# Two attentions on one core: output products one step behind a block's end, and the step with two maxima moved onto the block's end

## The chip, the core and the metric

The kernel runs on one core of a Trainium2 chip. The metric is device microseconds from launch to end. TensorE multiplies into PSUM, which has eight banks of 128 x 512 fp32; VectorE and ScalarE read PSUM and empty its banks; GpSimd works between tiles in SBUF; SyncE's queue issues almost all transfers. In the rows of a profile these are PE (PEld is the load of its weights), DVE, ACT, POOL and SP.

## What is computed

Two independent attentions over 2048 positions, each with 32 heads of 18 values (D = 576), in fp32. Attention A looks back at 8 positions, 2 apart; attention B looks at all. Their outputs stand side by side.

```python
def _A_ref(x, wqkv, wo):                      # H = 32, Dh = 18, W = 8, dil = 2
    q, k, v = ...                             # x @ wqkv, split by head
    idx = pos[:, None] - (jnp.arange(W) * dil)[None, :]
    logits = jnp.einsum("bhsd,bhswd->bhsw", q, k_at_idx) * scale
    logits = jnp.where(idx >= 0, logits, -1e9)
    o = jnp.einsum("bhsw,bhswd->bhsd", softmax(logits), v_at_idx)
    return o.reshape(B, S, D) @ wo

def _B_ref(x, wqkv, wo):
    scores = jnp.einsum("bhqd,bhkd->bhqk", q, k) * scale
    o = jnp.einsum("bhqk,bhkd->bhqd", softmax(scores), v)
    return o.reshape(B, S, D) @ wo

return jnp.concatenate([a, b], axis=-1)
```

## The kernel before

**Three stretches.** For some 416 us both attentions' queries, keys and values are projected; A's go to DRAM (`da`), B's queries and keys too (`dqk`), split into a rounded part and a remainder so that fast products keep fp32's precision. Then comes a main loop of 512 steps (`while step < ALL`), and in its last 25 steps most of B's output projection.

**A step of the main loop.** B's heads are taken in 8 groups of 4 (`g`), the queries of a group in 4 blocks of 512 (`b`), the keys in 16 tiles of 128 (`kt`). Step `step` is one tile: `step = 16 * block + kt`. It does the following.

- *Scores*: four products of keys and queries, one per head (line 388), each into a bank of PSUM, two of them into two neighbouring banks called `pair`. ScalarE takes the exponential of each (line 398) or of the pair at once (line 401).
- *Maxima*: the largest score of each query, which the exponential needs, is found for a later block. Three further products (line 239) fill three banks, one of them in two parts; VectorE reduces each by one instruction (lines 256, 258 and 272). A block has 64 maxima to be taken. When the last of them is taken, two small instructions of VectorE (lines 282 and 290) put them into order.
- *Values*: `weigh` multiplies the exponentials of the *previous* step with the values (line 898), four heads side by side in the bank `po`. These four are the last that a step has on TensorE.

Scores and maxima use 64 rows of TensorE each and run in two halves side by side; the value products use all 128 rows.

**A block's end.** The value products of a block's last tile (kt = 15) stand at the end of the step behind it, which is kt = 0 of the next block. There `finish` has VectorE copy `po` into `o` (line 908). The value products of the next step (kt = 1) start `po` anew, so they wait for that copy. One step later SyncE's queue loads the denominators (`den<-o`, line 932), and further steps divide and store.

**Attention A in between.** A's eight pieces are worked out by GpSimd, some instructions of VectorE (maxima `am`, line 1059, four per piece) and ScalarE (exponents, line 1069, one whole or two halves), beside B's steps. Piece `j` starts at step 10 + 55 j; some 90 steps later it is stored to `dao`. Some steps then load half of a piece back (`at` and `ahl`, lines 1118 and 1120) and multiply it with A's output weights (line 1239): these are the *output products*. There are 27 of them in a step, into two banks; ScalarE copies one bank to `y` and VectorE adds the other (line 1142). A loaded half serves two steps with products. The tile `at` has one buffer, so the next load waits until the products on it are done.

**Which steps have products.** `TURNS` is a sorted list of steps at which products may stand: one in every block (`16 * n + AT`), one for each piece's exponents, and the eight in `MORE`. Each half takes the next two free turns; its load is issued 9 steps ahead of the first, or as soon as the buffer's last step with products is over. The steps taken are kept in the set `producing`. Exponents are taken in one piece if their step has products, and in two halves, the first one step earlier, if not.

**How many maxima.** `many` is 3 as a rule. A step with products takes two more. A step next to a block's end without products takes two only. Three and no products is the *plain* step, whose order is fixed (`PLAIN`); a step with products or with two maxima has its order set by `in_turn`, which plays two queues, one per half of TensorE's rows, against expected times of the engines. `behind()` raises `many` to 4 if the maxima come late; here it never does.

**Order.** The order of the instructions on each engine is the order in which the code issues them; no scheduler moves them. Each engine waits on semaphores where an operand or a buffer isn't ready. SyncE's queue is served in order too, so a transfer that waits holds up those behind it.

Of the kernel before, what the change touches and what calls it, by code (L numbers as in the profile page):

```python
# [40 lines left out]
EARLY_PAIRS = EARLY * NB * PIECES + 8  # L41
AHEAD = 7

AT = 0

MORE = (439, 441, 451, 467, 475, 477, 484, 486)

# [7 lines left out]

TURNS = sorted({NT * n + AT for n in range(1, 30)} | {A_FROM + GAP * j + 35 for j in range(NJ)} | set(MORE))

# [12 lines left out]
def two_attentions(ctx: ExitStack, tc, xa, wa, woa, xb, wb, wob, out):  # L70
# [45 lines left out]
    def pooled(apart_):  # L116

        nonlocal ring
        ring = "pool"
        n = 7 if apart_ else 5  # L120
        if apart_:
            pair_room()
            freed[5] = freed[6] = freed["pair"]
        rings.update({k: list(range(n)) for k in ("pool", "scores", "else")})

    def apart():

        nonlocal ring
        ring = "else"
        assert not held  # L130
        if len(rings["else"]) == 7:
            pair_room()
            freed["pair"] = max(freed[5], freed[6])
        n = sorted(range(5), key=lambda i: freed[i])
        rings["scores"] = [n[1], n[3]]
        rings["else"] = [n[0], n[2], n[4]]
# [44 lines left out]
    step = 0  # L181
# [8 lines left out]
    def due():  # L190
        for f in agenda.pop(step, []):
            f()
# [126 lines left out]
    given = [0, 0]  # L319
    projecting = True  # L320

    def maximum(r):

        given[r] += 1
        return blocks[find(lambda rest: rest[r])][1](r)
# [14 lines left out]
    def first_part(r):  # L340

        for i in range(2):
            given[i] += 0.5
        if open_parts:
            part, args = open_parts.pop()
        else:
            rest, _, part = blocks[find(lambda rest: rest[0] and rest[1] and rest[0][-1][0] > 1)]
            piece = rest[0].pop()
            assert rest[1].pop() == piece
            args = (0, *piece)  # L350
            open_parts.append((part, (1, *piece)))
        ps = bank()
        ins, _ = part(*args, r, ps)
        taken = rings[ring][-1]

        def second():
            if ring == "else":
                rings["else"].remove(taken)
                rings["else"].append(taken)
            return part(*args, 1 - r, ps, ins)[1]  # L360

        return second
# [7 lines left out]
    def score(g, b, kt, h, kind):  # L370

        assert (g, b) in placed
        qs, ks = sets[g % 3]
        p, r = divmod(h, 2)
        at = slice(64 * r, 64 * r + 56)
        if len(scored) == 4:
            scored.clear()
            counted[0] += 1
        parity = counted[0] % 2
        n = sum(k == kind for k in scored)  # L380
        scored.append(kind)
        if kind == "pair":
            if n == 0:
                both_scores[:] = [pair_of_banks()]
            ps = both_scores[0][:, 512 * n : 512 * n + 512]
        else:
            ps = bank("else" if projecting else "scores")
        nc.tensor.matmul(ps, ks[at, p, 128 * kt : 128 * kt + 128], qs[at, b, p], start=True, stop=True)  # L388
        filled(r, 226, ps if kind != "pair" else None if n else both_scores[0])
        if kind == "single":  # L390
            e = whole = (work if parity else e_room).tile([128, 512], F32, name=f"e{n}{parity}", bufs=1)
        else:
            if n == 0:
                both_es[:] = [e_room.tile([128, 1024], F32, name=f"ee{parity}", bufs=1)]
            whole = both_es[0]
            e = whole[:, 512 * n : 512 * n + 512]
        if kind != "pair":
            nc.scalar.activation(e, ps, AF.Exp, scale=SCALE)  # L398
            emptied("ACT", 490, r, ps)
        elif n:  # L400
            nc.scalar.activation(whole, both_scores[0], AF.Exp, scale=SCALE)  # L401
            emptied("ACT", 916, r, both_scores[0])
        return e
# [102 lines left out]
    def do_all(fs):  # L506
        for f in fs:
            f()
# [6 lines left out]
    with (tc.tile_pool(name="x", bufs=1, side="right") as xp,  # L515
# [367 lines left out]
        step = 0  # L883
# [106 lines left out]
    producing = set()  # L990
# [254 lines left out]
    def in_turn(queues):  # L1245

        while any(queues):
            at = []
            for r, q in enumerate(queues):
                need = q[0][0] if q else None  # L1250
                free = 0
                if need == "E":
                    free = parted_at[0]
                elif need == "pair":
                    free = 0 if "pair" in held else freed["pair"] + 165
                elif need:
                    free = min(freed[i] for i in rings[ring] if i not in held) + 165 if any(i not in held for i in rings[ring]) else 1e9
                at.append(max(busy[r], free) if q else 2e9)
            r = int(at[1] < at[0])
            busy[0], busy[1] = max(busy[0], at[r]), max(busy[1], at[r])  # L1260
            queues[r].pop(0)[1]()
# [109 lines left out]
    total = early + rest  # L1371

    def behind():

        most = 0
        for n in range(int(sum(given)) // (2 * PIECES), NG * NB):
            until = NT * n - AHEAD
            more = 3 * (until - step) + 2 * sum(step <= p < until for p in producing)
            most = max(most, 2 * PIECES * (n + 1) - int(sum(given)) - more)
        return most  # L1380
# [4 lines left out]
    while step < ALL:  # L1385
        n, kt = divmod(step, NT)
        g, b = divmod(n, NB)
        many = min(4 if behind() > 0 else 2 if kt == 1 and step > 1 and step - 1 not in producing else 3, total - int(sum(given)))
        if open_parts and total - int(sum(given)) < 3:
            many = 1  # L1390
        es = [None] * 4
        products = inside.pop(0)() if inside else ([], [])
        plain = many == 3 and not any(products)
        if not plain:
            pooled(any(products))
        parts = many == 3 or many == 1 and open_parts
        left = many - parts
        a = left // 2 if left != 1 or given[0] >= given[1] else 1
        b_ = left - a
        extra = any(products) and int(sum(given)) + many + 2 <= total  # L1400
        ops = {"D": lambda: parted.append(first_part(0)) or parted_at.insert(0, busy[0] + 250), "E": lambda: parted.pop()()(),
               "A": lambda: maximum(0)(), "B": lambda: maximum(1)(),
               "+": lambda: None,
               **{c: lambda h=i % 4, kind="single" if i < 4 else "apart" if any(products) else "pair": es.__setitem__(h, score(g, b, kt, h, kind))
                  for i, c in enumerate("0123wxyz")}}

        def queue(text, own):
            q = []
            for c in text:
                if c == "+":  # L1410
                    q += own
                    own = []
                elif c == "p":
                    q += own[:1]
                    own = own[1:]
                else:
                    q.append((c if c == "E" else "pair" if c in "wxyz" and not any(products) else True, ops[c]))
            return q

        if plain:  # L1420
            do_all(ops[c] for c in PLAIN)
        elif any(products):
            in_turn([queue(ROWS[0].replace("D", "D" * parts).replace("A", "A" * min(a, 1)).replace("X", "A" * extra), products[0]),
                     queue(ROWS[1].replace("E", "E" * parts).replace("B", "B" * min(b_, 1)).replace("X", "B" * extra), products[1])])
        else:
            in_turn([queue("D" * parts + "0y" + "A" * a, []), queue("x" + "E" * parts + "B" * b_ + "3", [])])
        for fs in (behind_scores, outside):
            while fs:
                fs.pop(0)()

        if not plain and not paired and int(sum(given)) < total:
            apart()
        paired = paired or kt % 2 == 0 and int(sum(given)) == total
        for _ in range(1 if paired and step < ALL - 2 else len(waiting)):
            if waiting:
                waiting.pop(0)()
        if ready and (kt % 2 == 0 or not paired):
            weigh(ready.pop(0))
        ready.append((g, b, kt, es))
        if paired and kt % 2:  # L1440
            weigh(*ready)
            ready.clear()
        due()

        if len(waiting) > (0 if not paired else 2 if kt % 2 else len(waiting)):
            waiting.pop(0)()
        step += 1
# [24 lines left out]
```

## Time and profile before

| | us |
|---|---|
| median of 3 runs | 1587.92 (1584.57 to 1588.29) |
| the profiled execution | 1584.54 |
| its span, first to last instruction | 1582.7 |
| TensorE busy | 1571.9 (99%) |
| VectorE busy | 1399.5 (88%) |
| ScalarE busy | 1183.0 (75%) |
| GpSimd busy | 966.0 (61%) |

The profile's rows give start (us from the span's start), duration, engine, line of the code, operation, what it writes and reads, and how often it stands there in a row. Rows of groups give busy time in us and the mean of one in ns. A bracket gives the engine's idle time ahead of the row and what ended it. A matmul's recorded start is when it was taken up; where it has to wait for its bank, its duration is longer. Rows of a stretch give its bounds, its length, and for PE, PEld, DVE, ACT and POOL the busy time with the number of instructions, then the granted clock of TensorE, the share of the DMA engines that was busy, and GB/s. Each value product (fp32) has two rows in the profile.

### The profile page before, as it was taken

How to read it: one execution, taken by the hardware profiler on the slowest of the kernel's cores; microseconds unless marked ns; L12 is line 12 of the kernel's file. 1: busy time of each engine (PE TensorE's matmuls, PEld its weight loads, DVE VectorE, ACT ScalarE, POOL GpSimd, SP SyncE). 2: the span in 40 equal slices, each digit the busy share in tenths (PEclk: the TensorE clock that was granted, in tenths of full speed). 3: DMA queues.
4: the chain of work that ended last, by engine and by line, in shares of the span. 5: the costliest groups of instructions: out<-in, count | busy, mean ns of one | idle time of the engine just before them, and what ended most of it. 6: DMA issues, size and time to landing. Idle time of an engine off the chain costs nothing.

```text
span 1582.7 us, 34698 instructions
## 1 busy us (share of the span) xinstructions
PE 1571.9 (99%) x13400; PEld 949.5 (60%) x13400; DVE 1399.5 (88%) x2381; ACT 1183.0 (75%) x1916; POOL 966.0 (61%) x820
## 2 busy tenths in 40 slices
PE   9999999999999999999999999999999999999998
PEld 7999998888544444454444445444444445455776
DVE  5299999999999999999999999999999999999433
ACT  7323441211799999999998999999999999998444
POOL 2305752201267997994995995995995997940100
PEclk9999999999999999999999999999999999999999
DMA  8848964523322253253236225423613232234211
GB/s 260 222 130 210 260 183 123 161 81 93 75 56 55 64 114 95 65 139 104 58 85 170 58 67 142 96 54 105 141 56 92 67 86 79 62 124 158 85 39 61
DMA packets 190149, 173.12 MB, mean 109 GB/s; under 512 B 123120, under 2 KB 136944, under 8 KB 188256
## 3 DMA queue, kind: packets, MB, share of 16 engines
q1 hardware_dynamic: 185120, 159.36, 36.4%
q0 software_dynamic: 4032, 10.63, 3.2%
q8 instruction: 105, 1.72, 0.5%
q10 hardware_dynamic: 832, 0.92, 0.2%
q14 instruction: 60, 0.49, 0.1%
HBM read 97.47 MB, written 72.95 MB: 108 GB/s over the span
## 4 chain that ended last, share of the span: by engine, by line
PE 93%; DVE 2%; DMA 2%; issue 1%; POOL 1%; ACT 1%; SPq 0%; POOLq 0%; ACTq 0%; DVEq 0%
PE po L898 30%; PE bank L239 20%; PE bank L498 14%; PE bank L388 9%; PE bank L1239 8%; PE pair L388 7%; PE bank L424 4%; DVE mx L256 1%; DMA ks<-dqk 1%; POOL xlo L546 1%; DMA qs<-dqk 0%; DMA at<-dao 0%; DVE mx L272 0%; DVE o L908 0%; PE bank L664 0%
## 5 line engine op out<-in xcount | busy, mean ns | idle before, releaser
L239 PE MATMUL bank<-ks,qs 54*128 54x256 f32 (+1 forms) x2526 | 756.1, 373 | 1.2 <-DVE mx L256 0.5
L256 DVE TENSOR_REDUCE mx<-bank 128x1 f32<-128x512 f32 x1024 | 680.3, 684 | 60.7 <-PE bank L239 36.2
L239 PEld LDWEIGHTS bank<-ks,qs 54*128 54x128 f32 x2526 | 414.9, 184 | 427.5 <-DVE mx L272 308.3
L398 ACT ACTIVATE e<-bank 128x512 f32<-128x512 f32 x1024 | 610.9, 602 | 75.5 <-PE bank L388 68.6
L898 PE MATMUL po<-ee,v 128*19 128x512 f32 x2048 | 536.9, 599 | 1.0 <-DVE o L908 0.2
L898 PE MATMUL po<-e,v 128*19 128x512 f32 x2048 | 531.5, 599 | 0.0
L401 ACT ACTIVATE ee<-pair 128x1024 f32<-128x1024 f32 x478 | 487.5, 1020 | 0.3
L388 PE MATMUL bank<-qs,ks 56*128 56x512 f32 x1092 | 461.1, 442 | 0.0
L258 DVE TENSOR_REDUCE mx<-bank 128x2 f32<-128x512 f32 x546 | 356.1, 685 | 19.1 <-PE bank L239 6.9
L272 DVE TENSOR_REDUCE mx<-bank 128x2 f32<-128x512 f32 x478 | 326.1, 682 | 0.0
L388 PE MATMUL pair<-qs,ks 56*128 56x512 f32 x956 | 248.5, 396 | 0.0
L388 PEld LDWEIGHTS bank<-qs,ks 56*128 56x128 f32 x1092 | 194.6, 184 | 15.4 <-ACT e L398 8.3
L1090 POOL TENSOR_TENSOR pr<-lg,akv 128x1024 f32<-128x1024 f32 x72 | 157.0, 2201 | 0.6
L840 ACT ACTIVATE ohi<-bank 128x512 f32<-128x512 f32 (+1 forms) x56 | 30.6, 595 | 148.6 <-issue 126.3
L388 PEld LDWEIGHTS pair<-qs,ks 56*128 56x128 f32 x956 | 138.3, 186 | 0.0
L898 PEld LDWEIGHTS po<-ee,v 128*19 128x19 f32 x2048 | 69.8, 97 | 111.3 <-issue 107.4
L498 PE MATMUL bank<-xhi,ahi 64*128 64x512 f32 x448 | 114.6, 391 | 0.2 <-ACT ohi L843 0.2
L498 PE MATMUL bank<-xlo,ahi 64*128 64x512 f32 (+1 forms) x448 | 102.7, 392 | 0.2 <-POOL xlo L546 0.2
L498 PE MATMUL bank<-xhi,alo 64*128 64x512 f32 x416 | 101.0, 391 | 0.0
L1042 POOL TENSOR_TENSOR pr<-aq,akv 128x1024 f32<-128x1024 f32 x40 | 87.8, 2200 | 17.2 <-PE bank L239 16.0
L1092 POOL TENSOR_TENSOR pr<-pr 128x512 f32<-128x512 f32 x72 | 91.2, 1289 | 0.6
L652 POOL TENSOR_TENSOR olo<-olo,ohi 128x512 fp32r<-128x512 f32 x36 | 46.1, 1294 | 65.7 <-ACT ohi L651 61.3
(210 smaller groups left out, 2346.2 us busy)
## 6 DMA issues: line engine op xcount, KB each, us to landing
do<-n SPq DMA_DIRECT2D x28, 512.0 KB
da<-ohi SPq DMA_DIRECT2D x52, 256.0 KB
akv<-da SPq DMA_DIRECT2D x64, 175.5 KB
out<-y SPq DMA_DIRECT2D x32, 288.0 KB
qs<-dqk SPq DMA_DIRECT2D x30, 288.0 KB
ks<-dqk SPq DMA_DIRECT2D x30, 288.0 KB
at<-dao SPq DMA_DIRECT2D x64, 128.0 KB
rec<-drec SPq DMA_DIRECT2D x29, 256.0 KB
```

The source lines that it names most:

```text
L239: return nc.tensor.matmul(ps, qs[rows_, b, p, 128 * t : 128 * t + 128], ks[rows_, p, 512 * k + at : 512 * k + at + n], start=True, stop=True)
L256: nc.vector.tensor_reduce(mx[:, r, p, t, k : k + 1], ps, axis=AX.X, op=ALU.max)
L258: nc.vector.tensor_reduce(mx[:, r, p, t, 2 * k - 2 : 2 * k], ps.rearrange("q (h n) -> q h n", h=2), axis=AX.X, op=ALU.max)
L272: nc.vector.tensor_reduce(mx[:, :, p, t, 2 * k - 2 + i], ps.rearrange("q (h n) -> q h n", h=2), axis=AX.X, op=ALU.max)
L388: nc.tensor.matmul(ps, ks[at, p, 128 * kt : 128 * kt + 128], qs[at, b, p], start=True, stop=True)
L398: nc.scalar.activation(e, ps, AF.Exp, scale=SCALE)
L401: nc.scalar.activation(whole, both_scores[0], AF.Exp, scale=SCALE)
L498: nc.tensor.matmul(ps, a, b, start=start, stop=stop)
L898: nc.tensor.matmul(po[32 * i : 32 * i + 19], vs[g][:, kt, 19 * i : 19 * i + 19], es[i], start=kt == 0, stop=kt == NT - 1)
L1090: nc.gpsimd.tensor_mul(at, ap(st["lg"], (0, 2), (SUB, W), (1, SUB)), window(st["v"], n))
L1092: nc.gpsimd.tensor_add(at[:, :, :4], at[:, :, :4], at[:, :, 4:])
L1239: nc.tensor.matmul(sums_[r], a, b, start=i == 0, stop=i == len(both[r]) - 1)
```

## The change

Two lines differ.

```diff
-AT = 0
+AT = 1
...
-        many = min(4 if behind() > 0 else 2 if kt == 1 and step > 1 and step - 1 not in producing else 3, total - int(sum(given)))
+        many = min(4 if behind() > 0 else 2 if kt == 0 and step + 1 not in producing and step not in producing else 3, total - int(sum(given)))
```

`AT` moves the turn of every block from kt = 0, the step that ends with the previous block's last values, to kt = 1, the step behind it. The second line moves the step with two maxima from kt = 1 to kt = 0 of the blocks whose end has no products.

Which steps have products follows from the list of turns. In both kernels it is 33 steps. Of them 21 stand at kt = 0 before (112, 128, 144, 176 and so on up to 464); now 20 stand at kt = 1 (113, 129, 145, 177 and so on up to 465), and step 320 still has products, since it is also the step of a piece's exponents. Three other steps change: those at 210, 375 and 432 are gone, and there are some at 439 and 441; the one at 257 is followed by 265, whose load now stands at step 258, and 273. Steps with two maxima before are 17, 33, 49, 65, 81, 97, 161, 273 and 481; now they are 16, 32, 48, 64, 80, 96, 160, 432 and 480. (Step 488 has two in both, as the maxima run out.) As steps 210 and 375 have no products, the exponents of two pieces are taken in halves.

The order on VectorE at the first block end (step 16), where no products stand. `bank` is a bank of PSUM with its running number, `mx` the maxima, `o` the copy of `po`. Before:

```order
L258 TENSOR_REDUCE mx<-bank_6509 128x2
L258 TENSOR_REDUCE mx<-bank_6524 128x2
L272 TENSOR_REDUCE mx<-bank_6518 128x2
L258 TENSOR_REDUCE mx<-bank_6539 128x2
L908 COPY o<-po 128x512
L282 TENSOR_REDUCE m_82<-mx 128x16
L256 TENSOR_REDUCE mx<-bank_6561 128x1
L256 TENSOR_REDUCE mx<-bank_6564 128x1
L290 STREAM_TRANSPOSE mt<-m_82 128x32
```

And now:

```order
L258 TENSOR_REDUCE mx<-bank_6509 128x2
L258 TENSOR_REDUCE mx<-bank_6527 128x2
L258 TENSOR_REDUCE mx<-bank_6530 128x2
L908 COPY o<-po 128x512
L256 TENSOR_REDUCE mx<-bank_6552 128x1
L272 TENSOR_REDUCE mx<-bank_6545 128x2
L256 TENSOR_REDUCE mx<-bank_6567 128x1
L282 TENSOR_REDUCE m_82<-mx 128x16
L256 TENSOR_REDUCE mx<-bank_6584 128x1
```

The copy had three reductions of its own step ahead of it and two behind it; now it has two ahead and three behind.

VectorE at the first block end with products, which stood in step 112 and stand in step 113 now; `y` is the sum of the output products. Before:

```order
L256 TENSOR_REDUCE mx<-bank_9565 128x1
L256 TENSOR_REDUCE mx<-bank_9568 128x1
L272 TENSOR_REDUCE mx<-bank_9555 128x2
L256 TENSOR_REDUCE mx<-bank_9588 128x1
L256 TENSOR_REDUCE mx<-bank_9598 128x1
L1142 TENSOR_TENSOR y<-bank_9574,y 128x288
L908 COPY o<-po 128x512
L256 TENSOR_REDUCE mx<-bank_9637 128x1
L272 TENSOR_REDUCE mx<-bank_9631 128x2
L256 TENSOR_REDUCE mx<-bank_9652 128x1
```

And now:

```order
L256 TENSOR_REDUCE mx<-bank_9556 128x1
L272 TENSOR_REDUCE mx<-bank_9550 128x2
L256 TENSOR_REDUCE mx<-bank_9571 128x1
L908 COPY o<-po 128x512
L256 TENSOR_REDUCE mx<-bank_9598 128x1
L256 TENSOR_REDUCE mx<-bank_9601 128x1
L272 TENSOR_REDUCE mx<-bank_9588 128x2
L256 TENSOR_REDUCE mx<-bank_9621 128x1
L256 TENSOR_REDUCE mx<-bank_9631 128x1
L1142 TENSOR_TENSOR y<-bank_9607,y 128x288
```

The copy stood behind the five reductions and the sum of the step with products; now it stands ahead of them.

SyncE's queue at step 257, where the loads of the next group's queries and keys (`qs`, `ks`, 12 transfers) begin. Before:

```order
L306 DMA qs_1608<-dm 2x1024 x2
L216 DMA qs_88<-dqk 18x8x512 x2
L932 DMA den<-o 128x1x16
L216 DMA qs_88<-dqk 18x8x512 x4
L215 DMA ks_89<-dqk 18x2x2048 x6
L1108 DMA dao<-aohi 128x1152
```

And now:

```order
L306 DMA qs_1608<-dm 2x1024 x2
L216 DMA qs_88<-dqk 18x8x512 x2
L932 DMA den<-o 128x1x16
L1118 DMA at_14672<-dao 128x4x64 x2
L1120 DMA ahl<-dao 64x2x64
L1118 DMA at_14676<-dao 128x4x64 x2
L1120 DMA ahl<-dao 64x2x64
L216 DMA qs_88<-dqk 18x8x512 x4
L215 DMA ks_89<-dqk 18x2x2048 x4
L1179 DMA out<-y 128x576
```

The loads for the products of steps 265 and 273 moved into these transfers, ahead of ten of the twelve; before they stood ten steps earlier in the queue.

## The prediction

> **What bounds the kernel now.** I read the page first, then who waited for whom over the run, then the instructions in order of time at three kinds of block end.
>
> ```profile
> PE 1571.9 (99%) x13400; PEld 949.5 (60%) x13400; DVE 1399.5 (88%) x2381; ACT 1183.0 (75%) x1916; POOL 966.0 (61%) x820
> PE 93%; DVE 2%; DMA 2%; issue 1%; POOL 1%; ACT 1%; SPq 0%; POOLq 0%; ACTq 0%; DVEq 0%
> L256 DVE TENSOR_REDUCE mx<-bank 128x1 f32<-128x512 f32 x1024 | 680.3, 684 | 60.7 <-PE bank L239 36.2
> PEld po L898 <- DVE o L908: 9.1, 30, 0.5
> 640.00:1476.00 836.00, 833.95 (x7018) 408.62 (x7014) 790.87 (x1355) 771.29 (x1203) 655.68 (x519) 1.00 0.36 96
> ```
>
> TensorE works 99% of the span and carries 93% of the chain that ended last. The last row is the stretch that holds every moved step with products: TensorE is busy 834 of 836 us, VectorE 791. So VectorE has little room, and where it falls behind, TensorE finds a bank not yet emptied. That wait hardly shows as idle time; it shows as a longer step. I therefore measure steps: from one group of value products (L898, the end of a step) to the next.
>
> ```profile
> 777.40 0.61 PE L898 MATMUL po<-ee,v 128*19 128x512 f32 x1
> 781.48 0.61 PE L898 MATMUL po<-ee,v 128*19 128x512 f32 x1
> 783.48 0.61 PE L898 MATMUL po<-e,v 128*19 128x512 f32 x2
> 785.21 0.50 PE L239 MATMUL bank<-ks,qs 54*128 54x512 f32 x1
> 785.64 0.61 PE L898 MATMUL po<-ee,v 128*19 128x512 f32 x1
> 787.64 0.61 PE L898 MATMUL po<-ee,v 128*19 128x512 f32 x1
> ```
>
> This is TensorE at the block end of step 176. The step with products takes 4.08 us (777.40 to 781.48), the next 2.00, the one after 2.16, then 2.00 again. A plain step is thus 2.00, and the third is 0.16 too long. Its last maximum (785.21) lasts 0.50. VectorE at the same place tells why:
>
> ```profile
> 779.15 1.29 DVE L256 TENSOR_REDUCE mx<-bank 128x1 f32<-128x512 f32 x2 [0.24 <-PE bank L239]
> 782.15 0.45 DVE L1142 TENSOR_TENSOR y<-bank,y 128x288 f32<-128x288 f32 x1
> 782.67 0.69 DVE L908 COPY o<-po 128x512 f32<-128x512 f32 x1
> 783.27 0.68 DVE L256 TENSOR_REDUCE mx<-bank 128x1 f32<-128x512 f32 x1
> 783.87 0.68 DVE L272 TENSOR_REDUCE mx<-bank 128x2 f32<-128x512 f32 x1
> 784.47 1.36 DVE L256 TENSOR_REDUCE mx<-bank 128x1 f32<-128x512 f32 x2
> ```
>
> The copy that ends the block (0.69) comes behind the sum of the products (0.45), in a plain step. Reductions start 0.60 apart, so three and the copy need 2.4 us of a 2.0 us step. VectorE's spare time in a plain step is the 0.24 of the first row. The reduction started at 784.47 leaves its bank only at 785.15, where TensorE wants it at 785.21 less the load of its weights.
>
> **The change, part by part.** Nothing is added or removed: in both kernels 33 steps have products and ten steps have two maxima, so their base cost cancels. What moves is where the copy falls.
>
> *Twenty block ends with products.* Before, the copy lands in the plain step behind the products; now the block ends in a plain step and the copy lands at the start of the step with products. The price of the old place, at the first and the last of the twenty:
>
> ```profile
> 645.53 0.61 PE L898 MATMUL po<-e,v 128*19 128x512 f32 x2
> 647.60 0.61 PE L898 MATMUL po<-ee,v 128*19 128x512 f32 x1
> 1414.28 0.61 PE L898 MATMUL po<-e,v 128*19 128x512 f32 x2
> 1416.41 0.61 PE L898 MATMUL po<-ee,v 128*19 128x512 f32 x1
> ```
>
> The late step takes 2.07 at the first and 2.13 at the last, 2.16 in the middle (above): on average 0.12 over 2.00, 20 x 0.12 = 2.4 us to win. What does the copy cost in its new place? In the step with products VectorE has five reductions and one sum: 5 x 0.60 + 0.52 = 3.52 of 4.08 us, spare 0.56. A copy there makes its first reduction about 0.3 late (it can start only when the plain step's third reduction is out of the way), less than the spare. TensorE also has 27 products to do meanwhile. Bounds: 0, and 0.35 per step, what the one step with products that opens with a late VectorE shows (step 210, below). I take 0 for nineteen, since the five reductions' banks are then wanted over 3 us instead of 2, and 0.2 for step 209, where VectorE also has the local attention's maxima. Net -2.2.
>
> *Nine block ends without products.* Here the step with two maxima stands behind the block's end and now stands at it.
>
> ```profile
> 446.60 0.61 PE L898 MATMUL po<-ee,v 128*19 128x512 f32 x1
> 448.04 0.68 DVE L908 COPY o<-po 128x512 f32<-128x512 f32 x1
> 448.78 0.60 PE L898 MATMUL po<-ee,v 128*19 128x512 f32 x1
> 450.79 0.61 PE L898 MATMUL po<-e,v 128*19 128x512 f32 x1
> 1450.85 0.61 PE L898 MATMUL po<-ee,v 128*19 128x512 f32 x1
> 1453.02 0.61 PE L898 MATMUL po<-ee,v 128*19 128x512 f32 x1
> ```
>
> The step with two maxima takes 2.18 (446.60 to 448.78), the last of the nine 2.17, although it has less work: the next block's value products wait for the copy, which runs 448.04 to 448.72 because three reductions go before it. This is the 9.1 us over 30 copies above. Moved, only two reductions stand ahead of the copy; it can start when the value products end (1.1 us after they start, as 782.67 to 781.48), and 0.17 x 9 = 1.5 us goes. What is late next: the plain step behind it now has copy and three reductions, the situation of the twenty before, 0.07 to 0.16 in the step that follows; I take 0.09, for there is no sum ahead of the copy, 9 x 0.09 = 0.8. Net -0.7, bounds -1.5 and 0.
>
> *Two steps with products that are late.* Rows of TensorE and, last, SyncE:
>
> ```profile
> 846.11 0.61 PE L898 MATMUL po<-ee,v 128*19 128x512 f32 x1
> 849.05 0.40 PE L1239 MATMUL bank<-wohi,at 64*128 64x288 f32 x2 [1.11 <-DMA at<-dao]
> 850.08 0.40 PE L1239 MATMUL bank<-wohi,at 64*128 64x288 f32 x2 [0.62 <-DMA at<-dao]
> 852.43 0.60 PE L898 MATMUL po<-ee,v 128*19 128x512 f32 x1
> 854.43 0.61 PE L898 MATMUL po<-e,v 128*19 128x512 f32 x2
> 858.87 0.60 PE L898 MATMUL po<-ee,v 128*19 128x512 f32 x1
> 817.72 0.61 SPq L932 DMA_DIRECT2D den<-o  x1
> 828.28 4.98 SPq L215 DMA_DIRECT2D ks<-dqk  x4
> 835.22 2.73 SPq L1118 DMA_DIRECT2D at<-dao  x2
> 844.53 3.64 SPq L1120 DMA_DIRECT2D ahl<-dao  x1
> ```
>
> Step 208 takes 6.32 (846.11 to 852.43), 2.24 more than 4.08, waiting for the loads of `at`. They stand in SyncE's queue behind the next group's query and key loads, and these behind the den load of step 193, which waits for the copy at that block's end until 817.72. With the copy ahead of the products of step 193, den is free about 2 us sooner, and the products move from 208 to 209, 2 us later: some 4 us of room for a wait of 2.24. So -2.2, bounds 0 and -2.24. Step 210 takes 4.44 (854.43 to 858.87) since it follows the copy of step 208's block end and a local maximum at once. It moves to 225: -0.35. The load for the products of 265 moves ahead of ten query and key loads; behind it stand only transfers for a group whose first maxima are taken more than 60 steps later, so I cost it at nothing. If that cover fails it would show as another wait like 208's.
>
> *The local attention's exponents.* Two of the eight change from one piece under a step with products to two halves in front of it, because steps 210 and 375 have no products now.
>
> ```profile
> L1069 ACT ACTIVATE lg<-lg x10: 427/642/644, 504.7 to 1336.2; 128x512 f32<-128x512 f32 x6, 128x256 f32<-128x256 f32 x4
> ```
>
> A half is 0.43 against 0.64 whole: 2 x 0.21 more ScalarE time in all. Below: 0. Above: two halves each in the way, 4 x 0.43 = 1.7. I take +0.4, the added time.
>
> Sum: -2.2 - 0.7 - 2.2 - 0.35 + 0.4 = -5.05. The profiled execution took 1584.54 (span 1582.7 and 1.8 around it), so 1579.5 for one like it. It lies at the fast end: the median 1587.92 is 3.4 above. What the other runs spend more no row tells; a wait like 208's may be part. I put the median of the changed kernel 1.5 above the sum, **1581.0**; on this footing no change at all is 1586.0.
>
> **The rivals.** *The step with products pays.* TensorE's two row halves are interleaved ahead of time, and a late VectorE unbalances them. Speaks for it: step 210, 4.44. Against: there VectorE was behind by a copy, a local maximum and a transpose, not by a copy alone. At 0.35 for all twenty it is 20 x 0.35 - 0.2 = 6.8 more, 1587.8, slower than before's footing. It decides from 0.25 per step (5.05 / 20); from 0.5 the kernel is slower by more than 0.3%.
>
> *The loads of `at` are still late*, at 209 or at 265: another 2.2, 1583.2. For it: the loads took from 835.22 to 848.17 to be issued. Against: 4 us more room, and at 265 only two of the query loads go first.
>
> *VectorE is the bound, so order inside it is worth nothing.* Three reductions of 0.68 are 2.05 us, more than a plain step's 2.00. If each began only when the last had ended, VectorE would set every step, and both kinds of block end would cost the same in any order. Only 208 and 210 would gain: 1586.0 - 2.2 - 0.35 = 1583.4. The Trainium skill, "VectorE: DVE Perf Modes", section "The DRAIN you can't avoid", says that the next operation does not start until the pipe is empty, which is this case. The trace disagrees: 783.27 and 783.87 are 0.60 apart at 0.68 each, and VectorE sat idle 0.24 before 779.15.
>
> **How the numbers follow.** 0.3% is 4.8 us here, about what this kernel's measurement can tell from no change. My forecast has 0.60, a step with products that pays 0.16, late loads 0.14, VectorE as the bound 0.10. Range 1576.5 to 1588.0: below, all late steps at 0.16 and nothing given back (20 x 0.16 + 1.5 + 2.2 + 0.35 = 7.3, and 2 for waits that other runs may lose); above, the first rival. Against 1587.92, 1583.2 is the edge of faster. The forecast lies 2.2 inside it, four in five: 0.48; of late loads and bound about a third: 0.08. Slower needs the first rival at its worst or more waits on loads: 0.08. Faster 0.56, same 0.36, slower 0.08.
>
> **What would show it.** Right: at the twenty ends the steps take 2.0, 4.1, 2.0 with the copy ahead of the five reductions; the step with two maxima takes 2.0 instead of 2.18; no row of L1239 waits for `at`; the wait of L898 for L908 falls well under 9.1. Wrong: steps with products over 4.3 at block ends, a `DMA at<-dao` wait at 209, 241 or 265, or a step behind the two maxima that is as long as 2.18.

## The result, and the profile after

| | before | changed |
|---|---|---|
| median, side by side | 1585.6 us (1584.49 to 1588.29, 6 runs) | 1580.55 us (1580.31 to 1580.93, 6 runs) |
| ratio | | 0.9964, 95% interval 0.9954 to 0.9975 |
| profiled execution | 1584.54 | 1580.53 |
| its span | 1582.7 | 1578.7 |
| until the first value products | 416.55 | 416.31 |
| main loop, first to 488th group of value products | 1059.23 | 1055.70 |
| from there to the last group | 95.19 | 95.17 |

The changed kernel is 0.36% faster, 5.05 us by the medians and 4.0 by the two profiled executions. Of these, 3.53 lie in the main loop, where the steps were moved.

The page of the changed kernel: busy time of the engines, the chain that ended last, the group of single maxima.

```profile
PE 1570.7 (99%) x13400; PEld 950.1 (60%) x13400; DVE 1397.6 (89%) x2381; ACT 1183.5 (75%) x1918; POOL 966.0 (61%) x820
...
PE 96%; POOL 2%; DMA 1%; DVE 1%; issue 1%; ACT 0%; SPq 0%; POOLq 0%; ACTq 0%; DVEq 0%
...
L256 DVE TENSOR_REDUCE mx<-bank 128x1 f32<-128x512 f32 x1024 | 679.9, 684 | 59.5 <-PE bank L239 33.5
```

Its list of waits (us in total, times, longest), and the stretch that holds the moved steps:

```profile
PEld po L898 <- DVE o L908: 2.2, 9, 0.3
```

```profile
640.00:1476.00 836.00, 835.90 (x7054) 408.68 (x7054) 790.69 (x1359) 774.67 (x1209) 655.53 (x518) 1.00 0.36 97
```

Every engine has as many instructions as before (ScalarE two more). TensorE's waits for VectorE's copy fell from 9.1 us at 30 block ends to 2.2 at 9. Most of this is a change of name: ahead of the value products the load of weights stands idle for some 0.25 us in every step, and the list puts 512 of these down to `issue` now (126.7 us), where it was 492 (121.7 us). The row of waits `PE bank L1239 <- DMA at<-dao` is gone.

The instructions of the changed kernel at the block end of step 176, in order of time, TensorE's value products and VectorE:

```profile
776.71 0.61 PE L898 MATMUL po<-ee,v 128*19 128x512 f32 x1
...
778.72 0.61 PE L898 MATMUL po<-ee,v 128*19 128x512 f32 x1
...
780.15 0.68 DVE L908 COPY o<-po 128x512 f32<-128x512 f32 x1
780.75 1.28 DVE L256 TENSOR_REDUCE mx<-bank 128x1 f32<-128x512 f32 x2
...
782.79 0.60 PE L898 MATMUL po<-ee,v 128*19 128x512 f32 x1
```

The block now ends in a plain step of 2.01 us; the copy (780.15) opens the step with products, which takes 4.07, and the next takes 2.00. Over sixteen such ends (all but 208, 240, 272 and 384, which have more to them) the three steps average 2.01, 4.09 and 2.01, where they were 4.09, 2.01 and 2.17. The late step is gone and nothing took its place.

The same at step 16, a step with two maxima, which now ends its block (the block's last value products start at 446.35):

```profile
446.21 1.29 DVE L258 TENSOR_REDUCE mx<-bank 128x2 f32<-128x512 f32 x2 [0.33 <-PE bank L239]
446.35 0.61 PE L898 MATMUL po<-ee,v 128*19 128x512 f32 x1
...
447.54 0.69 DVE L908 COPY o<-po 128x512 f32<-128x512 f32 x1
...
448.15 0.68 DVE L256 TENSOR_REDUCE mx<-bank 128x1 f32<-128x512 f32 x1
448.36 0.60 PE L898 MATMUL po<-e,v 128*19 128x512 f32 x1
...
449.34 0.68 DVE L256 TENSOR_REDUCE mx<-bank 128x1 f32<-128x512 f32 x1
...
450.08 0.50 PE L239 MATMUL bank<-ks,qs 54*128 54x512 f32 x1
...
450.51 0.60 PE L898 MATMUL po<-ee,v 128*19 128x512 f32 x1
```

The copy starts when the block's value products are done, and the next step (446.35 to 448.36) has its 2.01. But the step after it, 448.36 to 450.51, has 2.15. VectorE sat idle 0.33 us *ahead* of the copy, where that time is of no use to it; behind the copy it has three reductions, the last of them (449.34) ends at 450.02, and TensorE's maximum at 450.08 lasts 0.50. Over eight of the nine ends the four steps averaged 2.01, 2.18, 2.00 and 2.01 before and 1.98, 2.03, 2.16 and 2.03 now: 8.20 and 8.19 together. (The ninth moved from 273 to 432.)

Two places lost time. First step 209, rows of VectorE and, last, TensorE:

```profile
848.88 0.68 DVE L908 COPY o<-po 128x512 f32<-128x512 f32 x1
849.48 0.37 DVE L1059 TENSOR_REDUCE am<-lg 128x16 f32<-128x128 f32 x1
849.77 0.20 DVE L290 STREAM_TRANSPOSE mt<-m 128x32 f32<-128x32 f32 x1
849.89 1.24 DVE L256 TENSOR_REDUCE mx<-bank 128x1 f32<-128x512 f32 x2
...
851.62 0.60 PE L898 MATMUL po<-ee,v 128*19 128x512 f32 x1
```

From 847.20 it takes 4.43: copy, local maximum and transpose stand ahead of its maxima. Before, 4.44 stood at 210. Then step 427, 2.67 where it was 2.08: the first local maximum of piece 7 waits for GpSimd's sum, at the head of VectorE's queue, with three reductions behind it.

```profile
1316.83 1.28 POOL L1049 TENSOR_TENSOR lg<-pr 128x512 f32<-128x512 f32 x1
...
1318.14 0.39 DVE L1059 TENSOR_REDUCE am<-lg 128x16 f32<-128x128 f32 x1 [0.49 <-POOL lg L1049]
...
1320.82 0.61 PE L898 MATMUL po<-ee,v 128*19 128x512 f32 x1
```

### The profile page after: what moved, and what is told of

Same layout as the page of the kernel before. It is cut to its first block, busy times and chain, and to the rows that moved or that the text cites. A ratio compares the mean times of both kernels' runs of the same rounds, so it can differ in the third digit from the quotient of the medians.

```text
span 1578.7 us, 34691 instructions
## 1 busy us (share of the span) xinstructions
PE 1570.7 (99%) x13400; PEld 950.1 (60%) x13400; DVE 1397.6 (89%) x2381; ACT 1183.5 (75%) x1918; POOL 966.0 (61%) x820
## 4 chain that ended last, share of the span: by engine, by line
PE 96%; POOL 2%; DMA 1%; DVE 1%; issue 1%; ACT 0%; SPq 0%; POOLq 0%; ACTq 0%; DVEq 0%
PE po L898 31%; PE bank L239 19%; PE bank L498 16%; PE bank L388 10%; PE bank L1239 8%; PE pair L388 7%; PE bank L424 4%; POOL pr L1045 1%; POOL aohi L1042 0%; DMA first<-xb 0%; DMA raw<-wa 0%; DVE mx L256 0%; POOL ks L177 0%; POOL ohi L844 0%; DMA da<-ohi 0%
## 5 line engine op out<-in xcount | busy, mean ns | idle before, releaser
L546 POOL TENSOR_TENSOR alo<-raw,ahi 128x512 fp32r<-128x512 f32 x13 | 16.8, 1294 | 113.1 <-ACT ahi L545 111.8
```

## The experiments

Times are medians. The kernel before ran beside each group of experiments. It had 1586.35 (1583.12 to 1591.74, 33 runs) beside the two lines alone, the changed kernel again and the early load; 1586.77 (1584.59 to 1591.28, 13 runs) beside its second profile, the two kernels with the copy twice and the first shift of the maxima; and 1587.57 (1583.99 to 1593.31, 10 runs) beside the last two. "Main loop" is the stretch of the table above, in each kernel's profile.

### Each line of the change alone, and the whole again

Products one step later, two maxima left where they were:

```diff
-AT = 0
+AT = 1
...
-... 2 if kt == 1 and step > 1 and step - 1 not in producing else 3 ...
+... 2 if kt == 1 and step > 1 and step not in producing and step - 1 not in producing else 3 ...
```

> Products one step behind the block's end (AT = 1), but the step with two maxima left behind the end (kt = 1), as before. Theory (the gain is that of the products and of the loads for step 208; moving the two maxima is worth nothing, since the 0.17 us taken off their step comes back two steps later): within 0.5 us of the changed kernel, so 1580.0 to 1581.0; the steps with two maxima take 2.18 again and the step behind them 2.00. Rival (moving the two maxima brings the 0.7 us of the prediction): 1581.3 or more.

The other line alone: the two maxima at the block's end, `AT` left at 0.

```diff
-... 2 if kt == 1 and step > 1 and step - 1 not in producing else 3 ...
+... 2 if kt == 0 and step + 1 not in producing and step not in producing else 3 ...
```

> The step with two maxima moved onto the block's end (kt = 0), products left at kt = 0 (AT = 0). Theory: within 0.5 us of the kernel before, the wait of L898 for the copy falls from 9.1 us to about 7, the step two behind each such end takes 2.15 to 2.2, and step 208 still waits some 2 us for its loads. Rival (the prediction's -0.7, bounds -1.5 and 0): 0.7 to 1.5 us faster than before.

The changed kernel again, beside them:

> The changed kernel once more, beside the others on the same chip: 1580.0 to 1581.0 in every run.

| | median us | ratio to before, 95% | main loop |
|---|---|---|---|
| products alone | 1581.29 (12 runs) | 0.9970 (0.9958 to 0.9981) | 1055.52 |
| two maxima alone | 1586.42 (12 runs) | 0.9998 (0.9988 to 1.0007) | 1059.34 |
| both | 1581.10 (10 runs) | 0.9966 (0.9955 to 0.9978) | 1055.85 |

The first line is the whole gain, the second is worth nothing that the runs can tell. The medians alone don't decide against the rival of the products alone: 1581.29 lies 0.01 short of its 1581.3, and the changed kernel, forecast at 1580.0 to 1581.0 in every run, had 1581.10 and single runs up to 1585.56. The main loops decide, for there the products alone lose nothing against both. TensorE's value products at the first step with two maxima, with the products moved alone:

```profile
452.85 0.60 PE L898 MATMUL po<-ee,v 128*19 128x512 f32 x1
...
455.03 0.60 PE L898 MATMUL po<-ee,v 128*19 128x512 f32 x1
...
457.02 0.60 PE L898 MATMUL po<-e,v 128*19 128x512 f32 x1
```

And with the two maxima moved alone:

```profile
446.74 0.61 PE L898 MATMUL po<-ee,v 128*19 128x512 f32 x1
...
448.75 0.60 PE L898 MATMUL po<-e,v 128*19 128x512 f32 x1
...
450.90 0.60 PE L898 MATMUL po<-ee,v 128*19 128x512 f32 x1
```

2.18 and 1.99 in the one, 2.01 and 2.15 in the other. The 0.17 moves by one step and stays. (The profiled run of the products alone is 6.3 us longer than the changed kernel's, all of it before the first value products: 422.80 against 416.31. The projections, the same in all kernels, can take that much longer in a single run. In this one TensorE's granted clock was 0.50 from 79.6 to 82.9, which by itself would cost 1.7 us at most (half of 3.4).)

### The loads of `at` for step 208, earlier

The kernel before, with this one load 16 steps ahead instead of 9:

```diff
-pieces.append((max(at + 1, one - 9) - start, lambda n=n: get(n)))
+pieces.append((max(at + 1, one - (16 if one == 208 else 9)) - start, lambda n=n: get(n)))
```

> The kernel before with one edit: the loads of at for the products of steps 208 and 210 are issued seven steps earlier (step 192's end instead of 199), ahead of the next group's query and key loads. Theory (2.2 us of the gain is the wait for these loads, and this wait is what differs from run to run of the kernel before): step 208 takes 4.1 instead of 6.3, the profiled execution is 2.0 to 2.3 us shorter than before's fastest, about 1582.3, and its runs lie within 0.7 us of each other where before's lie 3.8 apart. Rival (the spread has another source, or the wait only moves to a later transfer): the median gains under 1 us, or the runs still lie over 2 us apart.

1584.38 us (1581.93 to 1586.58, 12 runs), ratio 0.9980 (0.9969 to 0.9990). Step 208 fell from 6.32 to 4.11. In the profiled execution the main loop stayed at 1059.12, for step 214 grew by 1.64 and others by 0.1 and less. Its rows of SyncE's queue, GpSimd and VectorE there:

```profile
843.06 0.35 SPq L934 DMA_DIRECT2D drec<-den  x1
...
855.71 0.58 SPq L935 DMA_DIRECT2D rec<-drec  x1
...
862.05 1.28 POOL L936 TENSOR_TENSOR o<-o,rec 128x512 f32<-128x512 f32 x1 [6.80 <-DMA rec<-drec]
...
865.00 0.35 DVE L1080 RECIPROCAL as<-as 128x32 f32<-128x32 f32 x1 [1.73 <-POOL as L1076]
```

The load that went ahead put off the key loads behind it. These (the last issued from 835.65 to 841.06) were still under way when the denominators were to be stored (843.06); 9.8 us of the time to 855.71 is the next load's wait for that store. The trace's DMA packets show it: those of the key loads, 8 KB each, ran until about 854, and of the store's 128 packets 56 moved by 845, the others from 851 to 854.7. In the kernel before, the key loads were through by about 848, when the store was issued (848.26). GpSimd divides late, and VectorE waits for GpSimd's next work. So the wait could be moved, and by the medians 2.0 us were won on average, but its cause, the traffic around it, remained. My theory that the spread of the runs before is this one wait fell: these runs still spread over 4.6 us.

### The kernel before, a second profile

> The kernel before once more, for a second profile. My theory: its main stretch (first to 488th group of value products) is 1059.2 within 0.3 us again, and what its runs differ by lies in the first stretch, in the projections. Rival (the wait at step 208 is the part that varies): step 208 differs from 6.32 by over 0.5 us, and the main stretch with it.

One execution of 1587.09, main loop 1061.93, 2.70 longer than the first profile; before the first value products 416.41. TensorE's rows at step 208:

```profile
846.43 0.61 PE L898 MATMUL po<-ee,v 128*19 128x512 f32 x1
...
850.41 0.40 PE L1239 MATMUL bank<-wohi,at 64*128 64x288 f32 x2 [2.15 <-DMA at<-dao]
...
855.08 0.60 PE L898 MATMUL po<-ee,v 128*19 128x512 f32 x1
```

And its list of waits:

```profile
PE bank L1239 <- DMA at<-dao: 2.5, 2, 2.1
```

The rival holds: step 208 took 8.65 here and 6.32 in the first profile. It differs from run to run, by 2.33 of the 2.70 between these two. It isn't the only thing that does (the 422.80 above).

Only a third of the 2.33 is a longer wait. TensorE stood idle for 2.15 + 0.39 = 2.54 us here and for 1.11 + 0.62 = 1.73 in the first profile, 0.81 more. The other 1.5 came behind the wait: from the second idle time to the step's end the products took 3.88 us (851.20 to 855.08), where they had taken 2.35 (850.08 to 852.43). TensorE's granted clock, third from the end of the rows of these stretches, tells why. In the second profile, and then in the first:

```profile
851.30:854.70 3.40, 3.40 (x28) 3.40 (x29) 1.30 (x2) 0.00 (x0) 0.00 (x0) 0.51 0.74 268
```

```profile
849.00:852.50 3.50, 2.82 (x35) 2.40 (x39) 2.20 (x4) 0.30 (x1) 0.00 (x0) 1.00 0.67 229
```

For 3.4 us the clock was half. So a wait of TensorE can cost more than its length. It doesn't always: with the copy twice (below) the kernel before waited 1.63 + 0.52 us at this step, and the clock stayed at 1.00. No other main loop profiled here has such a stretch, and no run looked for what brings it on.

### The copy twice

To measure what a copy costs in the old place and in the new, it was made twice at the block ends with products, 22 copies more in each kernel (VectorE's instructions go from 2381 to 2403), 21 of them in the main loop. In the kernel before:

```diff
-nc.vector.tensor_copy(o, po)
+for _ in range(1 + (step in producing)):
+    nc.vector.tensor_copy(o, po)
```

> The kernel before, with the copy that ends a block made twice at the block ends with products; nothing else moves, and the output is the same. My theory (a plain step has 0.24 us of VectorE to spare, and what goes beyond it is paid step by step): the second copy, 0.60 us from start to start, has nothing to hide it, so each late step grows from 2.16 to about 2.7, and the twenty-odd ends cost 10 to 13 us. Rival (VectorE's queue is made up over the next steps, and the late step is an accident of the order): under 6 us.

In the changed kernel:

```diff
-nc.vector.tensor_copy(o, po)
+for _ in range(1 + (step in producing or step + 1 in producing)):
+    nc.vector.tensor_copy(o, po)
```

> The changed kernel, with the copy that ends a block made twice at the same block ends, where it now stands ahead of the step with products. My theory (that step has 0.56 us of VectorE to spare, and one copy of 0.60 uses it up): the first copy was hidden, the second is hidden only in part; the step with products grows from 4.12 by 0.2 to 0.45, so 4 to 9 us in all, clearly less than the same second copy costs in the kernel before. Rival one (VectorE is the bound, so a copy costs its 0.60 wherever it stands): 10 to 13 us, as in the kernel before. Rival two (the spare time is far more than 0.56): under 2 us, steps with products still 4.1.

| | median us | main loop | per end |
|---|---|---|---|
| before, copy twice | 1601.04 (2 runs) | 1075.01, +15.8 | 2.01 became 2.66, 2.17 became 2.24 |
| changed, copy twice | 1595.34 (3 runs) | 1067.30, +11.6 | 4.09 became 4.52, 2.01 became 2.16 |

Against the kernel before, the ratios are 1.0084 (1.0062 to 1.0106) and 1.0058 (1.0033 to 1.0083). Copy and value products of the kernel before with the copy twice, at the block end of step 176:

```profile
785.55 1.42 DVE L909 COPY o<-po 128x512 f32<-128x512 f32 x2
...
787.02 0.61 PE L898 MATMUL po<-e,v 128*19 128x512 f32 x2 [0.59 <-DVE o L909]
```

And of the changed kernel with the copy twice:

```profile
784.15 1.41 DVE L909 COPY o<-po 128x512 f32<-128x512 f32 x2
785.48 1.28 DVE L256 TENSOR_REDUCE mx<-bank 128x1 f32<-128x512 f32 x2
...
787.24 0.60 PE L898 MATMUL po<-ee,v 128*19 128x512 f32 x1
```

Both of my figures were too low, and in the old place it isn't the late step that grew but the one ahead of it. The second copy starts 0.73 behind the first (1.42 less 0.69), not 0.60, so 21 of them are 15.3 us of VectorE. In the old place they cost 15.8 (0.4 of it at step 208, whose wait varies), all of their time: the next value products wait for the copy directly (0.59). In the new place each costs 0.58: 0.15 is hidden. The total of 11.6 (with 0.6 won back at step 427 in it) falls among the figures of the first rival, but this rival (a copy costs its full time wherever it stands) is wrong for the first copy: the three steps together took 8.26 before and 8.11 now, against 8.08 without any delay (4.08 + 2 x 2.00; or 8.10, by the 4.09 to 4.10 of steps 265, 439 and 441, which stand away from a block's end). So the first copy costs 0.18 in the old place and 0.03 or less in the new, the second 0.73 and 0.58. Two copies ask 0.60 + 0.73 = 1.33 and are charged 0.61 in the new place, so the step with products and the plain step behind it hide some 0.7 us. One copy fits into that, two don't.

### The local attention's maxima, out of the way

The changed kernel, the four maxima of piece 3 three steps earlier, those of piece 7 one later:

```diff
-MOST = ((30, 0, 4), (31, 1, 4), (32, 2, 4), (33, 3, 4))
+shift = {3: -3, 7: 1}.get(j, 0)
+MOST = tuple((30 + shift + i, i, 4) for i in range(4))
...
-LOWER, SHARE, MATCH, WEIGHT = 33, 38, 5, 38
+LOWER, SHARE, MATCH, WEIGHT = 33 + max(shift, 0), 38, 5, 38
```

> The changed kernel, with the local attention's four maxima of piece 3 three steps earlier (202 to 205 instead of 205 to 208) and those of piece 7 one step later. My theory (what was given back at 209 is copy and local maximum together, and 427 waits for GpSimd's part of the same local attention): step 209 falls from 4.43 to 4.1 and step 427 from 2.67 to 2.1; the main stretch is 0.8 to 1.0 us shorter than the changed kernel's 1055.7 and the median 0.5 to 1.2 below it, near 1580.3. Step 241, which has no local attention near it, stays at 4.28. Rival (the two steps are late from the sum and the order of the products, not from these maxima): both stay, 0 us; or the wait for GpSimd shows at another step of piece 3 or 7.

1581.56 us (9 runs), ratio to before 0.9967 (0.9957 to 0.9977); main loop 1055.89. Both steps did as expected, 209 from 4.43 to 4.09 and 427 from 2.67 to 2.03, and 241 stayed at 4.27. But step 204 went from 2.01 to 3.01 and took it all back. GpSimd and VectorE there:

```profile
836.06 1.29 POOL L1049 TENSOR_TENSOR lg<-pr 128x512 f32<-128x512 f32 x1
...
837.39 0.40 DVE L1059 TENSOR_REDUCE am<-lg 128x16 f32<-128x128 f32 x1 [0.82 <-POOL lg L1049]
```

Three steps earlier, the maximum stands ahead of the sum that it reads. So once more, with piece 3 one step earlier only (`{3: -1, 7: 1}`), and the changed kernel beside it:

> The changed kernel, with the local attention's four maxima of piece 3 one step earlier and those of piece 7 one step later. Three steps earlier, the first of piece 3 had to wait 0.82 us for GpSimd's sum (done at 837.35, inside step 204) and step 204 grew by 1.0 us, which gave back what 209 and 427 gained. My theory (copy and local maximum together make 209 late, and nothing else): one step earlier the sum has long been done, so step 209 is 4.1 and 427 about 2.05 with nothing lost at 204 to 208, and the main stretch is 0.8 to 1.0 us below the changed kernel's 1055.7; the median is 0.5 to 1.2 below the changed kernel's in the same runs, which the spread of the runs may hide. Rival (VectorE is full over the whole stretch, so what is not paid at 209 is paid in steps 205 to 208): the main stretch stays within 0.3 of 1055.7.

> The changed kernel again, as the yardstick of the run before on the same chip. Both theories: main stretch 1055.7 within 0.3, step 209 4.43 and 427 2.67, median 1580.5 to 1582.

1580.07 us (1579.59 to 1582.36, 6 runs) against 1580.79 (1580.44 to 1581.59, 6 runs) of the changed kernel; ratios to before 0.9953 (0.9936 to 0.9970) and 0.9955 (0.9939 to 0.9972). The main loop is 1054.89 against 1055.55. Step 427 is 2.01 and only 0.1 is lost at 204 to 208, but 209 is still 4.26. VectorE there:

```profile
848.78 0.68 DVE L908 COPY o<-po 128x512 f32<-128x512 f32 x1
849.38 0.20 DVE L290 STREAM_TRANSPOSE mt<-m 128x32 f32<-128x32 f32 x1
849.51 1.25 DVE L256 TENSOR_REDUCE mx<-bank 128x1 f32<-128x512 f32 x2
```

The local maximum is gone from behind the copy, the transpose is not, and the copy itself comes 1.67 us behind the start of the value products (847.11), as late as in the changed kernel (848.88 less 847.20); at step 177 it is 1.43 (778.72 to 780.15, above): VectorE is still behind from the steps before. So the local maximum beside the copy is half of 209's lateness. But little of it is won: step 209 is 0.17 and step 210 0.13 shorter, 206 and 212 are 0.08 and 0.13 longer. For this stretch the rival, by which it is paid in other steps, is nearer than the theory, and nearly all that the main loop won is step 427's. With 0.7 us less in the trace this version is the shortest of all, by less than the runs can tell.

## Why the prediction was right, and where it wasn't

Forecast 1581.0, measured 1580.55; the sum for an execution like the profiled one was 1579.5, and the profiled one took 1580.53. Term by term, in the main loop:

| term | predicted | measured in the trace |
|---|---|---|
| twenty ends with products | -2.2 | -2.2: late steps -2.7, given back at 209 and 210 +0.5 |
| nine ends with two maxima | -0.7 | -0.1 |
| the wait at 208 | -2.2 | -2.2 |
| step 210 | -0.35 | -0.36 |
| exponents in halves | +0.4 | the rest, +1.3: 427 +0.6, other steps by 0.2 and less |
| sum | -5.05 | -3.5 |

**The twenty ends: right**, in mechanism and sum. The late step was worth more than I took (0.15 instead of 0.12: I averaged three ends, and the first and the last, 0.07 and 0.13, are among the lowest), and the giving back was more as well: 0.34 at 209, where I had 0.2, and 0.16 in the step behind. Step 241, at 4.28, gave 0.19 back (about as much as step 384 won, 4.25 before) for a reason that stays open; it did so in every kernel with the products moved, with the local maxima moved too, but not with the copy made twice, where it is 4.52 like its neighbours.

**The nine ends: wrong.** The step that failed is "the plain step behind it now has copy and three reductions, the situation of the twenty before, 0.07 to 0.16 in the step that follows; I take 0.09". It measured 0.07 to 0.18, and 0.37 at step 98, where a local maximum stands behind the copy too; with 0.155 on average it took back what was won: the two experiments with one line each show the same 0.17 in one place or the other. My reason for the low value, that no sum stands ahead of the copy, doesn't carry: what counts is what stands behind it. VectorE's idle time of such a step lies ahead of the copy, as the row at 446.21 shows (0.33 or 0.34 at six of the eight ends), and cannot be kept. At the ends with products the long step stands *behind* the copy, and there the spare time serves. Idle time behind a copy isn't enough by itself: in the kernel before, VectorE stood idle for 0.50 us behind the copy and the two maxima of step 33, and that step was late all the same, for its value products waited for the copy itself.

```profile
482.66 0.69 DVE L258 TENSOR_REDUCE mx<-bank 128x2 f32<-128x512 f32 x1 [0.50 <-PE bank L239]
```

**Step 208: right.** The rows of SyncE's queue in the changed kernel, and the first output product of step 209:

```profile
815.01 0.61 SPq L932 DMA_DIRECT2D den<-o  x1
...
832.17 2.79 SPq L1118 DMA_DIRECT2D at<-dao  x2
...
840.58 3.95 SPq L1120 DMA_DIRECT2D ahl<-dao  x1
...
848.99 0.55 PE L1239 MATMUL bank<-wohi,at 64*128 64x288 f32 x4
```

The `den` load is issued 2.7 us earlier than before (817.72), the loads are all issued at 844.53 instead of 848.17, and the first product on them starts at 848.99 without a wait. I said 2 us for `den` and 2 for the later step. It was 2.7 (3.6 by the end of the loads) and 1.1: the products wanted `at` at 847.94 before, 849.05 less the wait of 1.11, and at 848.99 now. These are times from the span's start, and the changed kernel is 1.0 us ahead at the end of step 207 (845.12 instead of 846.11); counted from the steps, the loads are done 2.6 earlier and the products stand 2.1 later, near what I said. No run moves one without the other. The load for step 265, costed at nothing, cost nothing.

**Step 210: right in size, but not a gain of its own.** Copy and local maximum met again at 209.

**The exponents: mis-sized, and under the wrong name.** What the trace shows isn't ScalarE's longer time: 427 is VectorE held by GpSimd, since the steps around piece 7 now come at other times than GpSimd's sum: it was done 0.66 us ahead of the start of step 427 before, and 0.03 ahead now. With the copy made twice this wait vanished by itself (step 427 at 2.08), so it is a coincidence of times that another edit undoes, though every run of the changed kernel that was profiled has it (2.58 to 2.67). Of the other small steps (122, 269, 358, 377 and 445, about 0.2 each, against 151, 373, 267 and 270, which became shorter by 0.1 to 0.2) no cause was looked for.

**The footing.** I put 1.5 on top of the sum because the runs of the kernel before lie above its profiled one and "a wait like 208's may be part". The second profile shows that it is part: 2.33 us more at 208, most of it at half the clock. The changed kernel has no such wait; its six runs beside the result lie within 0.6 us, and their median is that of the profiled one, so the 1.5 wasn't needed. But ten later ones went from 1580.43 to 1585.56, so it has other things to lose time by. The medians moved by 5.05 and the two profiled executions by 4.0, as the one of before lies at the fast end of its runs. How much of their spread is step 208 isn't shown; it goes with the mean granted clock of a run, for of the 33 runs of before the 15 at 1.000 average 1585.1 and the 11 at 0.997 and 0.998 average 1588.8. The median of before that I was given, 1587.92, came out as 1585.6 with more runs.

That the forecast hit within 0.5 us is luck in part: the sum was 1.0 too low, the footing 1.5 too high, and the two errors nearly cancelled. What was right is where the time went: the late steps behind the copy, and the wait at 208.

**The rivals.** A step with products that pays at all twenty ends did not come about (4.09). But two of my signs of being wrong did show: one step with products over 4.3 (209, at 4.43), and steps behind the two maxima as long as 2.18 (50 and 98). No load was late. VectorE as the bound of every step, by the Trainium skill's "VectorE: DVE Perf Modes", section "The DRAIN you can't avoid", would have left only the two single places, 2.55; the trace disagrees again: at 448.15, 0.61 us behind a copy of 0.69, the next reduction had begun. This fits what the same section adds, that a next operation that isn't held starts earlier.

## What to carry to other kernels

An engine that is nearly full has spare time only where it is idle *behind* the burden: put a burst of work ahead of the long step, not after it, and not behind a step whose idle time is already past. This helps only if nothing waits for the burst itself. Shifting a burst between two steps that both lack such room only moves the loss, and one kernel with each line of the edit alone shows it. When a transfer is late, look at the whole queue around it, since the load brought forward only pushes the next one back.

## What the runs showed that was not expected

Two copies from the same bank into the same tile started 0.73 us apart on VectorE, at 0.69 each, while a reduction behind a copy, or behind another reduction, started 0.60 after it where its bank was ready; an experiment that doubles an instruction thus costs more than one instruction. And a store of 8 KB to DRAM issued at 843.06, behind key loads of 288 KB each, held the load that waits for it 9.8 us; in the kernel before, that wait was 1.0. At other places of the kernel before the same wait lasts up to 8.9 us, so its length is nothing new, only its place. From the list of waits of SyncE's queue with the early load:

```profile
SPq L935 <- DMA drec<-den: 9.8, 1, 9.8
```

And in the kernel before:

```profile
SPq L935 <- DMA drec<-den: 1.0, 1, 1.0
```
